# Batch 0's scores formed twice and one exponential per part, batch 1's mask added by TensorE

## The chip, the cores and the metric

The kernel runs on one core of a Trainium2 chip. The metric is the device time of one execution in microseconds (us). Every time below comes from timed runs or from one profiled execution. PE is the matrix engine (TensorE), DVE is VectorE, ACT is ScalarE, POOL is GpSimd, SP issues the DMAs.

## The reference

Three parts follow each other. Only the first is touched by the change.

```python
# q, k, v: 4 batches x 8 heads x 576 positions x 64
scores = (1/8) * q @ k.T
# heads 0..3: keys within 32 positions before the query (local)
# heads 4..7: earlier keys with the same position modulo 32 (strided)
scores = np.where(mask, scores, -1e9)
scores = scores - scores.max(-1)
attn = np.exp(scores); attn /= attn.sum(-1) + 1e-9
x = (attn @ v)                       # becomes 2304 tokens x 512
...
h = x @ w_in                         # 512 x 2048
g = h * sigmoid(1.702 * h)
x = g @ w_out                        # 2048 x 512
...
# soft mixture: 8 experts of 4 slots each, over all 2304 tokens
```

## The kernel before, in words

**Attention.** Heads go in pairs, `hp` = 0 to 3; pairs 0 and 1 are local, 2 and 3 strided (with positions permuted so that the keys a query needs are dense). Every pair has two parts. `att_scores(b, hp, part)` forms one part's scores in one PSUM bank: 5 or 4 tiles of 96 keys for a local pair (480 or 384 columns), 6 or 5 tiles of 64 keys for a strided one (384 or 320 columns), each tile with two small f32 matmuls for the pair's heads (L162). Then DVE takes the negated maximum of each row (L175), ACT takes the exponential of each tile with that maximum as bias and sums its row (L180), DVE adds 1e-9 and inverts (L181, L182), and POOL multiplies (L183). Batches differ in the mask. In batch 0 (`early`) a bf16 matmul with the identity writes eight times the mask into the bank first (L155, L157) and the scores accumulate on it; the maximum and the exponentials read PSUM. In the other batches DVE scales the scores and adds the mask on the way to SBUF (L165). `att_transpose` transposes the probabilities on PE and copies them out, in batch 0 alternately by DVE (L200) and ACT (L202); `att_values` multiplies with the values and splits the result into two tensors for the next product (L242 on ACT, L243 on DVE).

**Order of attention.** `attention_steps(b)` gives scores of the first parts, then scores, transposes and values in turn. Batch 0 runs at the start, before the expert layer. After each of its score steps one filler matmul is issued, and four after each other step (`keep_busy`, L78: bf16, 512 columns, their result is not used). Batches 1, 2 and 3 run beside chunks 0, 1 and 2 of the layer that follows, one step at a time.

**The layer.** The 2304 tokens are cut into chunks of 512, 512, 512, 512 and 256. For each chunk, 16 steps `f` each form 128 hidden units by 12 matmuls (`gemm1`, L312) and their activation (L315 on ACT, L316 on DVE). In chunk 0 the weights come along: `load_w` (L260 on ACT, L261 on POOL, L262 to L264 on DVE) converts a pair of 64-bit tiles to f32 two steps ahead, `split` (L271 on ACT, L272 on POOL) cuts a weight into two parts, `wo_transpose` (L279) and `wo_phi` (L287) prepare the logits, which L331 forms. `load_w` for f = 0 and 1 and `split(0)` are issued within batch 0's attention. Conversion tiles have four buffers, raw tiles three; scores, transposes, values and several others share five PSUM banks (`ps_m`). After the chunks come the experts, whose 28 MB of weights are loaded when chunk buffers come free.

**Order on the engines.** Semaphores and the order of instructions on each engine come from a planner, which starts from the program's order and reorders by its own costs. An engine then executes its list in that order.

Of the kernel before, what the change touches and what calls it, by code (L numbers as in the profile page):

```python
# [13 lines left out]
AF = mybir.ActivationFunctionType  # L14
ALU = mybir.AluOpType
AX = mybir.AxisListType
# [12 lines left out]
SCALE = 0.125  # L29
# [12 lines left out]
def tile_kernel(ctx: ExitStack, tc: tile.TileContext, lqk, lv, sqk, sv, wraw, phi, wexp, cst, out):  # L42
    nc = tc.nc
    P = 128
# [20 lines left out]
    def mtile(name):  # L65
        return ps_m.tile([P, 512], F32, tag="m", name=name)
# [16 lines left out]
    ident = cs[:, C_ID:C_ID + 128]  # L83
# [3 lines left out]
    identb = att.tile([P, P], BF16, name="identb", bufs=1)  # L87
    maskb = att.tile([P, C_END - C_ML], BF16, name="maskb", bufs=1)
    maskL, maskL0, maskS = maskb[:, :KL], maskb[:, KL:2 * KL], maskb[:, 2 * KL:]
# [39 lines left out]
    def att_scores(b, hp, part):  # L129
        t = qkv[b, hp]  # L130
        local = hp < 2
        nk, step = (KL, QT) if local else (KS, QS)
        ko = S if local else SW
        total, half = (NTL, 5) if local else (NTS, HS)
        u0, u1 = (0, half) if part == 0 else (half, total)
        nt = u1 - u0
        early = b == 0
        nm = f"{b}_{hp}_{part}"
        if part == 0:
            shape = [P, NTL if local else 2 * HS, nk]  # L140
            if b == 0 and hp >= 2:
                ts = ep.tile(shape, F32, name=f"ts_{b}_{hp}")
            else:
                ts = att.tile(shape, F32, tag="ts", name=f"ts_{b}_{hp}")
            probs[b, hp] = ts
            if not local:
                nc.gpsimd.memset(ts[:, NTS], 0.0)
        if local:
            ts = probs[b, hp][:, u0:u1]
        else:  # L150
            ts = probs[b, hp].rearrange("p (j e) k -> p e j k", e=2)[:, part, :nt]
        sp = mtile(f"s_{nm}")[:, :nt * nk].rearrange("p (u k) -> p u k", k=nk)
        mask = maskL if local else maskS
        if early:
            nc.tensor.matmul(sp, identb, mask.unsqueeze(1).to_broadcast([P, nt, nk]), start=True, stop=False)  # L155
            if local and part == 0:
                nc.tensor.matmul(sp[:, 0], identb, maskL0, start=False, stop=False)  # L157
        for u in range(nt):
            qo = step * (u0 + u)
            for h in range(2):  # L160
                hs = slice(64 * h, 64 * h + 64)
                nc.tensor.matmul(sp[hs, u], t[hs, qo:qo + 64], t[hs, ko + qo:ko + qo + nk], start=not early, stop=not early or u == nt - 1)  # L162

        def add_mask(a, z, m):
            nc.vector.scalar_tensor_tensor(ts[:, a:z], sp[:, a:z], SCALE, m.unsqueeze(1).to_broadcast([P, z - a, nk]), op0=ALU.mult, op1=ALU.add)  # L165

        if not early:
            if local and part == 0:
                add_mask(0, 1, maskL0)
                add_mask(1, nt, mask)  # L170
            else:
                add_mask(0, nt, mask)
        nmx = att.tile([P, 6], F32, tag="nmx", name=f"nmx_{nm}", bufs=4)
        src, sc = (sp, SCALE) if early else (ts, 1.0)
        nc.vector.tensor_reduce(nmx[:, :nt], src, axis=AX.X, op=ALU.max, negate=True)  # L175
        if early:
            nc.vector.tensor_scalar_mul(nmx[:, :nt], nmx[:, :nt], SCALE)
        sm = att.tile([P, 6], F32, tag="sm", name=f"sm_{nm}", bufs=4)
        for u in range(nt):
            nc.scalar.activation(ts[:, u], src[:, u], AF.Exp, scale=sc, bias=nmx[:, u:u + 1], accum_out=sm[:, u:u + 1])  # L180
        nc.vector.tensor_scalar_add(sm[:, :nt], sm[:, :nt], 1e-9)  # L181
        nc.vector.reciprocal(sm[:, :nt], sm[:, :nt])  # L182
        nc.gpsimd.tensor_tensor(ts, ts, sm[:, :nt].unsqueeze(2).to_broadcast([P, nt, nk]), op=ALU.mult)  # L183

    def att_transpose(b, hp):
        ts = probs.pop((b, hp))
        local = hp < 2
        nk, groups = (KL, ((0, 3), (3, 6), (6, 9))) if local else (P, ((0, 3), (3, 6)))
        if b == 0 and hp % 2:
            pt = ep.tile([P, groups[-1][1], P], F32, name=f"pt_{b}_{hp}")  # L190
        else:
            pt = att.tile([P, groups[-1][1], P], F32, tag="pt", name=f"pt_{b}_{hp}", bufs=1)
        ptiles[b, hp] = pt
        for n, (a, z) in enumerate(groups):
            ptp = mtile(f"ptp_{b}_{hp}_{n}")[:, :P * (z - a)].rearrange("p (u q) -> p u q", q=P)
            for u in range(a, z):
                src = ts[:, u] if local else ts[:, 2 * u:2 * u + 2].rearrange("p e k -> p (e k)")
                nc.tensor.transpose(ptp[:nk, u - a], src, ident)  # L198
            if n % 2 == 0 and b == 0:
                nc.vector.tensor_copy(pt[:nk, a:z], ptp[:nk])  # L200
            else:
                nc.scalar.copy(pt[:nk, a:z], ptp[:nk])  # L202

    def att_values(b, hp):
        pt, v = ptiles.pop((b, hp)), vals[b, hp]
# [272 lines left out]
    def attention_steps(b):  # L478
        la = 2 if b else 4
        order = list(range(la)) + [x for u in range(la, 8) for x in (la - 1 - u, u)] + list(range(la - 9, -9, -1))  # L480
        for x in order:
            if x >= 0:
                if b and x % 2 == 0:
                    load_qk(b, x // 2)
                att_scores(b, x // 2, x % 2)
                if b == 0:
                    keep_busy(1)
            else:
                x = -x - 1
                if x % 2:  # L490
                    att_values(b, x // 2)
                else:
                    if b:
                        load_v(b, x // 2)
                    att_transpose(b, x // 2)
                if b == 0:
                    keep_busy(4)
            yield
# [286 lines left out]
```

## Time and profile before

| | |
|---|---|
| time, median of 3 runs | 447.37 us (446.51 to 449.94) |
| time of the profiled execution | 446.48 us |
| its span, first to last instruction | 444.7 us |
| busy: PE, DVE, ACT, POOL | 415.2, 264.7, 189.4, 77.6 us |
| granted TensorE clock, mean | 0.98 of full |

Busy times are sums over a core whose engines work side by side, and a matmul counts as busy until its modelled end, also when it is held up. The span is 1.8 us shorter than the time of the execution.

### The profile page before, as it was taken

Reading aid. Unit: us, or ns where it says so; the run is one execution under the profiler, and the core shown is the slowest. Engines: PE = TensorE matmul, PEld = TensorE weight load, DVE = VectorE, ACT = ScalarE, POOL = GpSimd, SP = SyncE. Lnnn points to the kernel's source line nnn. Section 1 sums busy time; section 2 is a strip of 40 time slices with the busy share of each in tenths; the row PEclk is TensorE's granted clock in tenths of the full one; section 3 lists DMA queues with packets and bytes.
Section 4 is the critical chain, followed back from the end, with each engine's and each line's share of the span. In section 5 each row is a group of like instructions: output and inputs, shape, how many; then the busy total and the mean of one; then the engine's idle time right before and its main releaser. Section 6 shows DMA issues by size and latency. Waiting matters only on the chain.

```text
span 444.7 us, 9668 instructions
## 1 busy us (share of the span) xinstructions
PE 415.2 (93%) x3896; PEld 287.2 (65%) x3902; DVE 264.7 (60%) x564; ACT 189.4 (43%) x619; POOL 77.6 (17%) x96
## 2 busy tenths in 40 slices
PE   8877999998879999999999999999999999699964
PEld 3655786766557776776675867875777797243533
DVE  2589999988876565545656556545545464622213
ACT  1885776766555553445462436331221222020212
POOL 0354454535451100010010001000000000010000
PEclk9999999999898999999999999999999999999995
DMA  8956667584762120212503101570001899999998
GB/s 233 364 163 220 243 183 271 172 314 148 251 199 65 57 76 23 91 35 64 185 1 97 34 5 38 182 291 1 1 0 44 336 357 310 363 346 425 420 386 281
DMA packets 23229, 80.88 MB, mean 182 GB/s; under 512 B 2064, under 2 KB 7056, under 8 KB 19088
## 3 DMA queue, kind: packets, MB, share of 16 engines
q1 hardware_dynamic: 23184, 80.26, 50.8%
q8 instruction: 31, 0.51, 0.5%
q14 instruction: 14, 0.11, 0.1%
HBM read 71.34 MB, written 8.91 MB: 180 GB/s over the span
## 4 chain that ended last, share of the span: by engine, by line
PE 71%; DMA 9%; DVE 8%; ACT 4%; POOL 4%; issue 2%; SPq 0%; ACTq 0%; POOLq 0%
PE h L312 42%; DMA ex<-wexp 7%; PE lg L331 5%; PE u L416 4%; PE s L162 4%; PE ptp L198 3%; PE wp L287 3%; PE av L217 2%; DVE wc L263 2%; ACT ts L180 2%; DMA qk<-lqk 2%; POOL wi L272 2%; PE wot L279 1%; POOL ts L183 1%; DVE wc L264 1%
## 5 line engine op out<-in xcount | busy, mean ns | idle before, releaser
L312 PE MATMUL h<-x,wi 128*128 128x512 f32 (+1 forms) x960 | 224.7, 381 | 5.9 <-POOL wi L272 3.5
L312 PEld LDWEIGHTS h<-x,wi 128*128 128x128 f32 x960 | 162.7, 190 | 53.5 <-issue 13.8
L316 DVE SCALAR_TENSOR_TENSOR gT<-gT,h 128x512 f32<-128x512 f32 (+1 forms) x64 | 40.5, 633 | 61.8 <-ACT gT L315 61.4
L315 ACT ACTIVATE gT<-h 128x512 f32<-128x512 f32 (+1 forms) x64 | 35.6, 556 | 69.7 <-PE h L312 69.5
L180 ACT ACTIVATE ts<-ts,nmx 128x64 f32<-128x64 f32 (+1 forms) x120 | 41.6, 349 | 29.5 <-DVE nmx L175 29.2
L183 POOL TENSOR_TENSOR ts<-ts,sm 128x384 f32<-128x384 f32 (+2 forms) x32 | 28.1, 880 | 139.5 <-DVE sm L182 65.4
L339 DVE STREAM_TRANSPOSE gT<-gT 128x512 f32<-128x512 f32 (+1 forms) x64 | 41.0, 649 | 0.8
L261 POOL TENSOR_SCALAR wc<-wc 128x512 f32<-128x512 f32 x32 | 24.3, 759 | 32.9 <-ACT wc L260 32.7
L263 DVE SCALAR_TENSOR_TENSOR wc<-raw,wc 128x512 uint32<-128x512 uint32 x32 | 28.0, 878 | 0.3
L264 DVE SCALAR_TENSOR_TENSOR wc<-raw,wc 128x512 uint32<-128x512 uint32 x32 | 26.7, 834 | 0.1
L331 PE MATMUL lg<-gT,wp 128*32 128x512 f32 (+1 forms) x128 | 26.4, 564 | 0.0
L162 PE MATMUL s<-qk 64*64 64x96 f32 (+1 forms) x552 | 24.8, 235 | 0.8 <-DMA qk<-lqk 0.8
L272 POOL TENSOR_TENSOR wi<-wc,wi 128x512 fp32r<-128x512 f32 x16 | 22.5, 1406 | 16.2 <-ACT wi L271 15.8
L162 PEld LDWEIGHTS s<-qk 64*64 64x64 f32 x552 | 20.9, 133 | 6.7 <-issue 4.7
L202 ACT COPY pt<-ptp 96x384 f32<-96x384 f32 (+1 forms) x34 | 15.1, 482 | 20.5 <-PE ptp L198 20.3
L262 DVE TENSOR_SCALAR wc<-wc 128x512 uint32<-128x512 uint32 x32 | 17.3, 544 | 10.6 <-POOL wc L261 10.5
L242 ACT CAST x<-av 128x320 fp32r<-128x320 f32 (+20 forms) x54 | 19.1, 399 | 10.3 <-DVE x L243 8.9
L181 DVE TENSOR_SCALAR sm<-sm 128x5 f32<-128x5 f32 (+2 forms) x32 | 7.1, 222 | 26.7 <-ACT ts L180 26.5
L180 ACT ACTIVATION_READ_ACCUMULATOR ts<-ts,nmx 128x1 f32 x120 | 22.6, 188 | 0.0
L198 PE MATMUL ptp<-cs,ts 128*96 128x128 f32 (+1 forms) x120 | 18.3, 286 | 4.1 <-POOL ts L183 3.0
L416 PE MATMUL u<-gT,dT 32*32 32x512 f32 x576 | 20.2, 597 | 1.9 <-DVE z L396 1.9
L260 ACT ACTIVATE wc<-raw 128x512 f32<-128x512 f32 x32 | 21.6, 679 | 0.2 <-DMA raw<-wraw 0.2
(112 smaller groups left out, 457.7 us busy)
## 6 DMA issues: line engine op xcount, KB each, us to landing
ex<-wexp SPq DMA_DIRECT2D x28, 1024.0 KB, 8.2
raw<-wraw SPq DMA_DIRECT2D x32, 512.0 KB, 3.9
qk<-lqk SPq DMA_DIRECT2D x8, 592.0 KB, 4.2
wo_scr<-wc SPq DMA_DIRECT2D x16, 256.0 KB, 2.4
ex<-wo_scr SPq DMA_DIRECT2D x4, 1024.0 KB, 6.9
gT<-wexp SPq DMA_DIRECT2D x4, 1024.0 KB, 5.9
out<-gT SPq DMA_DIRECT2D x8, 512.0 KB, 4.1
qk<-sqk SPq DMA_DIRECT2D x6, 604.0 KB, 4.2
```

The costliest lines, as they stand in the source:

```text
L162: nc.tensor.matmul(sp[hs, u], t[hs, qo:qo + 64], t[hs, ko + qo:ko + qo + nk], start=not early, stop=not early or u == nt - 1)
L180: nc.scalar.activation(ts[:, u], src[:, u], AF.Exp, scale=sc, bias=nmx[:, u:u + 1], accum_out=sm[:, u:u + 1])
L183: nc.gpsimd.tensor_tensor(ts, ts, sm[:, :nt].unsqueeze(2).to_broadcast([P, nt, nk]), op=ALU.mult)
L198: nc.tensor.transpose(ptp[:nk, u - a], src, ident)
L263: nc.vector.scalar_tensor_tensor(u, raw[:, :, 1], 0xC0000000, u, op0=ALU.bitwise_and, op1=ALU.bitwise_or)
L272: nc.gpsimd.tensor_tensor(w[:, 1], t, w[:, 0].bitcast(F32), op=ALU.subtract)
L312: nc.tensor.matmul(h[:, :N], w[:, we, 128 * kt:128 * kt + 128], x[xe][:, kt, :N], start=n == 0, stop=n == 11)
L315: nc.scalar.activation(g[:, :N], h[:, :N], AF.Tanh, scale=0.851)
L316: nc.vector.scalar_tensor_tensor(g[:, :N], g[:, :N], 1.0, h[:, :N], op0=ALU.add, op1=ALU.mult)
L331: nc.tensor.matmul(lgs[c][32 * j:32 * j + 32, :N], wp[:, f0 + j, :], gs[c, f0 + j][:, :N], start=f0 == 0, stop=f0 == NF - 4)
L339: nc.vector.transpose(t_slots(c)[:, f, :N], gs[c, f][:, :N])
L416: nc.tensor.matmul(us[a][32 * j:32 * j + 32, :].rearrange("p (t f) -> p t f", f=32), dT[q, 32 * b:32 * b + 32], gT[q, :, 32 * b:32 * b + 3 ...
```

## The change

In batch 0 (`whole`) a part's mask and scores are formed once for the maximum and then a second time into another bank, onto which a matmul with the f32 identity adds the negated maximum, spread over each tile's columns. ACT takes one exponential over the whole part, and DVE sums the rows. The eight small multiplications of the maximum by 1/8 leave batch 0. In batch 1 the mask is added by TensorE as batch 0 had it, and maximum and exponentials read PSUM; these parts get the small multiplication. In batches 1 to 3 the 1e-9 is added by POOL. All copies of transposed probabilities go to ACT.

```diff
-        early = b == 0
+        early, whole = b < 2, b == 0
...
+        def scores(name, last):
+            sp = mtile(name)[:, :nt * nk].rearrange("p (u k) -> p u k", k=nk)
+            if early:
+                nc.tensor.matmul(sp, identb, mask.unsqueeze(1).to_broadcast([P, nt, nk]), start=True, stop=False)
+                if local and part == 0:
+                    nc.tensor.matmul(sp[:, 0], identb, maskL0, start=False, stop=False)
+            for u in range(nt):
+                qo = step * (u0 + u)
+                for h in range(2):
+                    hs = slice(64 * h, 64 * h + 64)
+                    nc.tensor.matmul(sp[hs, u], t[hs, qo:qo + 64], t[hs, ko + qo:ko + qo + nk], start=not early, stop=not early or (last and u == nt - 1))
+            return sp
+
+        sp = scores(f"s_{nm}", True)
...
-        if early:
-            nc.vector.tensor_scalar_mul(nmx[:, :nt], nmx[:, :nt], SCALE)
         sm = att.tile([P, 6], F32, tag="sm", name=f"sm_{nm}", bufs=4)
-        for u in range(nt):
-            nc.scalar.activation(ts[:, u], src[:, u], AF.Exp, scale=sc, bias=nmx[:, u:u + 1], accum_out=sm[:, u:u + 1])
-        nc.vector.tensor_scalar_add(sm[:, :nt], sm[:, :nt], 1e-9)
+        if whole:
+            sp = scores(f"t_{nm}", False)
+            nc.tensor.matmul(sp, ident, nmx[:, :nt].unsqueeze(2).to_broadcast([P, nt, nk]), start=False, stop=True)
+            nc.scalar.activation(ts, sp, AF.Exp, scale=SCALE)
+            nc.vector.tensor_reduce(sm[:, :nt], ts, axis=AX.X, op=ALU.add)
+            nc.vector.tensor_scalar_add(sm[:, :nt], sm[:, :nt], 1e-9)
+        else:
+            if early:
+                nc.vector.tensor_scalar_mul(nmx[:, :nt], nmx[:, :nt], SCALE)
+            for u in range(nt):
+                nc.scalar.activation(ts[:, u], src[:, u], AF.Exp, scale=sc, bias=nmx[:, u:u + 1], accum_out=sm[:, u:u + 1])
+            nc.gpsimd.tensor_scalar_add(sm[:, :nt], sm[:, :nt], 1e-9)
...
-            if n % 2 == 0 and b == 0:
-                nc.vector.tensor_copy(pt[:nk, a:z], ptp[:nk])
-            else:
-                nc.scalar.copy(pt[:nk, a:z], ptp[:nk])
+            nc.scalar.copy(pt[:nk, a:z], ptp[:nk])
```

## Rows read from the trace of the kernel before

**Rows 1.** Windows: stretch, length; busy PE, PEld, DVE, ACT, POOL; clock; DMA.

```profile
6.69:20.00 13.31, 11.72 (x176) 8.09 (x178) 5.95 (x20) 9.57 (x50) 4.08 (x5) 1.00 1.02 350
20.00:42.67 22.67, 16.75 (x243) 11.60 (x241) 20.68 (x46) 16.02 (x62) 10.30 (x13) 1.00 0.60 195
42.67:100.00 57.33, 56.10 (x448) 41.33 (x447) 53.68 (x100) 39.38 (x123) 27.55 (x31) 1.00 0.69 237
100.00:144.42 44.42, 38.98 (x298) 27.92 (x300) 34.61 (x62) 24.13 (x69) 19.04 (x19) 0.92 0.51 166
144.42:344.00 199.58, 199.41 (x1804) 144.31 (x1804) 109.89 (x230) 80.91 (x275) 14.09 (x20) 1.00 0.20 67
```

**Rows 2.** Groups by line, 6.69 to 42.67 us: busy us, mean ns | idle before.

```profile
L180 ACT ACTIVATE ts<-s,nmx 128x64 f32<-128x64 f32 (+1 forms) x40 | 12.4, 347 | 1.6 <-DVE nmx L177 1.3 <-issue 0.2
L78 PE MATMUL busy<-busy 128*128 128x512 bf16 x33 | 9.1, 385 | 0.5 <-issue 0.3 <-PE av L217 0.2
L175 DVE TENSOR_REDUCE nmx<-s 128x5 f32<-128x480 f32 (+3 forms) x8 | 4.5, 561 | 5.1 <-PE s L162 5.1
L200 DVE COPY pt<-ptp 96x384 f32<-96x384 f32 (+1 forms) x6 | 3.3, 546 | 1.9 <-PE ptp L198 1.9
L177 DVE TENSOR_SCALAR nmx<-nmx 128x5 f32<-128x5 f32 (+2 forms) x8 | 1.7, 214 | 0.1
```

**Rows 3.** Timeline of PE and DVE in batch 0: start us, us.

```profile
6.69 0.37 PE L155 MATMUL s<-maskb,identb 128*128 128x480 bf16 x1
...
8.01 0.34 PE L155 MATMUL s<-maskb,identb 128*128 128x384 bf16 x1
...
8.27 0.88 PE L162 MATMUL s<-qk 64*64 64x96 f32 x16
...
25.53 0.30 PE L155 MATMUL s<-maskb,identb 128*128 128x320 bf16 x1
...
26.49 0.39 PE L78 MATMUL busy<-busy 128*128 128x512 bf16 x1
...
26.79 1.65 DVE L263 SCALAR_TENSOR_TENSOR wc<-raw,wc 128x512 uint32<-128x512 uint32 x1
...
28.36 0.48 DVE L175 TENSOR_REDUCE nmx<-s 128x5 f32<-128x320 f32 x1
...
31.46 0.43 DVE L262 TENSOR_SCALAR wc<-wc 128x512 uint32<-128x512 uint32 x1 [0.95 <-POOL wc L261]
...
31.92 0.69 DVE L263 SCALAR_TENSOR_TENSOR wc<-raw,wc 128x512 uint32<-128x512 uint32 x1
```

**Rows 4.** Groups by line, 42.67 to 144.42 us.

```profile
L165 DVE SCALAR_TENSOR_TENSOR ts<-s,maskb 128x384 f32<-128x384 f32 (+2 forms) x10 | 4.6, 476 | 3.6 <-PE s L162 3.6
...
L181 DVE TENSOR_SCALAR sm<-sm 128x5 f32<-128x5 f32 (+2 forms) x8 | 2.3, 293 | 0.1
```

**Rows 5.** The chain of waits from 122 us on: start us, us, what.

```profile
122.72 0.62 ACT wi L271
...
129.88 0.62 ACT wi L271
...
140.93 0.63 PE wot L279 x4
...
142.49 0.88 PE wp L287 x8
...
144.38 1.63 PE s L162 x36
146.01 2.95 PE h L312 x12
...
154.89 1.06 PE lr L380 x2
...
159.57 1.20 PE av L217 x36
...
172.87 1.12 PE ptp L198 x9
```

More of the change, by code (lines that the diff above doesn't have):

```diff
@@ L151, in att_scores @@
             ts = probs[b, hp].rearrange("p (j e) k -> p e j k", e=2)[:, part, :nt]
-        sp = mtile(f"s_{nm}")[:, :nt * nk].rearrange("p (u k) -> p u k", k=nk)
         mask = maskL if local else maskS
-        if early:
-            nc.tensor.matmul(sp, identb, mask.unsqueeze(1).to_broadcast([P, nt, nk]), start=True, stop=False)
-            if local and part == 0:
-                nc.tensor.matmul(sp[:, 0], identb, maskL0, start=False, stop=False)
-        for u in range(nt):
[L159 to L162, printed above, removed]
+        def scores(name, last):
[11 more added lines that the diff above has]
+        sp = scores(f"s_{nm}", True)
         def add_mask(a, z, m):
@@ L175, in att_scores @@
         nc.vector.tensor_reduce(nmx[:, :nt], src, axis=AX.X, op=ALU.max, negate=True)
-        if early:
-            nc.vector.tensor_scalar_mul(nmx[:, :nt], nmx[:, :nt], SCALE)
         sm = att.tile([P, 6], F32, tag="sm", name=f"sm_{nm}", bufs=4)
-        for u in range(nt):
-            nc.scalar.activation(ts[:, u], src[:, u], AF.Exp, scale=sc, bias=nmx[:, u:u + 1], accum_out=sm[:, u:u + 1])
-        nc.vector.tensor_scalar_add(sm[:, :nt], sm[:, :nt], 1e-9)
+        if whole:
[10 more added lines that the diff above has]
+            nc.gpsimd.tensor_scalar_add(sm[:, :nt], sm[:, :nt], 1e-9)
         nc.vector.reciprocal(sm[:, :nt], sm[:, :nt])
```

## The prediction

> **What bounds the kernel now.** I read the windows first, stage by stage [rows 1]. They split the run into four. From 6.69 us, where the first scores start, to 42.67 us, where the first expert-layer product (`gemm1` of chunk 0, f = 0) ends, no engine is full over the whole stretch: PE is busy 11.72 + 16.75 = 28.5 of 36.0 us, so 7.5 us idle; DVE idles until 20 us and is at 20.68 of 22.67 after it. From 42.67 to 144.42 us (chunk 0 with the weight conversion and batch 1's attention beside it) DVE is at 53.68 + 34.61 = 88.3 of 101.75 us and PE, on paper, at 95.1. From 144.42 to 344 us PE is full (199.4 of 199.6), and in the tail to 444.7 us the expert weights are loaded and used. The change adds work to PE in the first stage and takes work off DVE and ACT in the first two; chunks 1 to 4 only shift by what the first two stages lose or win, and so does the tail, whose loads start when chunk buffers come free. So the question is when chunk 0 ends.
>
> In the first stage the groups by line [rows 2] show what the change aims at: 40 exponentials of 347 ns on ACT, and six copies and eight reductions of about 0.55 us on DVE. They also show 33 filler matmuls (`keep_busy`, L78): these are issued in program order like all else, the change keeps them, and PE has to run them. So PE's slack is the 7.5 us of idle time and not the fillers.
>
> In chunk 0, "busy" overstates PE: a matmul that waits counts until it ends. A product of 12 matmuls takes 2.95 us alone [rows 5]. The chain of waits [rows 5] shows the pace there in two ways. Part of it runs through DVE's conversions; part is a loop: ACT's cast of a weight tile (122.72), POOL's subtraction, PE's product and `wo_phi`, and only then ACT's next cast (129.88), 7.16 us for one step with no DVE in it. The mean step is (144.42 - 42.67) / 15 = 6.78 us.
>
> **First stage, PE.** Each of batch 0's eight parts repeats its mask and scores and adds one f32 matmul with the identity. Scores, start to start [rows 3]: 8.01 - 6.69 = 1.32 us for the first local part, 26.49 - 25.53 = 0.96 us for the last strided one. The other two forms have 384 columns, between these; I put them at an estimated 1.1 us each. Twice the four forms: 2 x 4.48 = 9.0 us. The identity matmul is not in this trace. The nearest row is the f32 product of 512 columns with a 128x128 operand, two records in 1.06 us [rows 5]; the four forms have 480, 384, 384 and 320 columns, 1568 in all, and each comes twice: 2 x 1568 / 512 x 1.06 = 6.5 us. From below it is bounded by the single-record products of the expert layer, 2.95 / 12 = 0.246 us for 512 columns, which gives 1.5 us. I take 6.5, because the row at 154.89 has the same operand types as the new matmul. Added: 15.5 us. Against 7.5 us of idle time that leaves **+8.0 us** at the end of the first product, if PE fills every hole (low end 9.0 + 1.5 - 7.5 = +3.0).
>
> The new matmul waits for DVE's reduction, and matmuls queued behind it wait too. A reduction takes 0.561 us on average [rows 2], less than the repeated scores of 0.96 to 1.32 us, so these cover it where DVE is free. For the last part it was not [rows 3]: the scores were out at about 26.49, a conversion of 1.65 us stood in front (26.79), the reduction ran from 28.36 to 28.84. That is 2.35 us against a cover of 0.96, so 1.4 us of parking. For the seven others I estimate some 0.6 us together, from the same stage's DVE being less full before 20 us. Up to 2.0 us in all; I take none, because DVE has fewer copies and a conversion may go earlier, and keep +10.0 as the high end.
>
> **First stage, ACT and DVE.** ACT loses 40 exponentials (12.4 us, and the reads of their sums) and gains eight of up to 480 columns; its cast of 512 columns takes 0.62 us [rows 5], so at most about 8 x 0.62 = 5.0 us, and six copies, which took 0.546 us on DVE. That is some 4 us or more off ACT, all beside a PE that is now the later engine: worth nothing by itself, but it lets the first casts of raw weights go earlier. DVE loses six copies (3.3 us) and eight small multiplications (1.7) and gains eight sums over the same shapes as the maxima (4.5 us for eight): -0.5 us, nothing. The first exponential moves behind the first identity matmul, by the repeat and that matmul some 2.3 us; this lies under the scores that PE still has to do.
>
> **Chunk 0.** Batch 1 loses ten mask additions on DVE, 4.6 us, and eight additions of 1e-9, 2.3 us [rows 4]; it gains eight multiplications of 0.214 us [rows 2], 1.7 us. DVE: **-5.2 us**, at full worth where DVE sets the pace. The 1e-9 goes to POOL, which is idle more than half of this stage (27.55 + 19.04 = 46.6 of 101.75 us). There it queues behind conversions, but POOL's next multiplication of the same part had to wait for the same exponentials anyway, so little new waits. PE gains ten mask matmuls: 8.27 - 8.01 = 0.26 us each [rows 3], 2.6 us. From the chain, a step needs 2.95 + 0.63 + 0.88 us, 15 of them 66.9; attention of one local pair 1.63 + 1.20 + 1.12 = 3.95, four pairs at most 15.8; I allow 3 us for logits. That is 85.7 of 101.75 us, 16 us of slack, and the 2.6 us lie in it. If that cover is gone, they count.
>
> A score bank of batch 1 is now held until its exponentials are done instead of until the mask is added, some 2 us longer by a reduction of 0.561 and up to six exponentials of 0.347 us [rows 2], out of five banks; nothing in the chain waits for a bank by name, so I cost it at nothing.
>
> **Head start.** With ACT free earlier and PE late, one more weight pair can be converted before the first product. DVE needs for each of its two tiles 0.43 us (31.46) and 0.69 us twice (31.92; the third operation is of the same form) [rows 3], 3.6 us for the pair; the four buffers of the conversion allow one such pair. Between 0 and -3.6 I take half: **-1.8 us**.
>
> **Batches 2 and 3** only send the 1e-9 through POOL. They run under a PE that is full [rows 1]; nothing.
>
> The sum is made against the profiled execution, whose time was 446.48 us with a span of 444.7: 446.5 + 8.0 - 5.2 - 1.8 = **447.5 us**. The median of the runs, 447.37, is 0.9 above that execution, the same within what it can tell: a change of under 1%, 442.9 to 451.8, can't be told from none.
>
> **Rivals.** *Slower: the lost time is never won back.* The place is the loop of 7.16 us through ACT's cast and POOL's subtraction. If it, and not DVE, sets most of chunk 0's steps, 5.2 us off DVE buy nothing and the first stage's high end stands: 446.5 + 10.0 = 456.5 us; should the masks fall into the loop, 2.6 more. It decides once the step stays at 6.78 us or more. For it: between 100 and 144.42 us DVE is at only 34.61 of 44.42 us. Against: from 42.67 to 100 us it is at 53.68 of 57.33 [rows 1]. On the parking in it the Trainium skill has a rule (TensorE: Matmul & The Clock Gate, "The mechanism"): matmuls start and end in program order, only weight loads are pulled ahead, so nothing that is ready behind a waiting identity matmul can pass it. By that rule the 2.0 us are lost in full, 449.5 us in place of the sum's 447.5 if the rest holds; no run here shows such a matmul yet.
>
> *Faster: chunk 0 runs at PE's pace.* PE then needs 85.7 + 2.6 = 88.3 us from 42.67 + 8.0 = 50.7, so chunk 0's last product ends at 139.0 instead of 144.42: 446.5 - 5.4 = 441.1 us, and down to 436 with the cheap identity matmul. It decides if the step falls below about 6.2 us. For it: DVE then has 83 us of work in 88. Against: the loop, and two nearly full engines feeding each other.
>
> *The change doesn't do what it says:* if the new instructions end up in an order in which PE idles as before in the first stage, the 15.5 us count nearly whole, and it is the slow case or worse.
>
> **How the numbers follow.** Forecast 0.42, with its own range 446.5 + 3.0 - 5.2 - 3.6 = 441 to 446.5 + 10.0 - 5.2 = 451; the fast rival 0.30, the slow one 0.28. Of the forecast's 0.42 some 0.04 lie below 442.9 and 0.01 above 451.8: faster 0.34, same 0.37, slower 0.29. Leaving one in ten off either end gives 438 to 457.
>
> **What would show it.** The first product's tanh at about 50.7 us instead of just after 42.67; PE idle under 2 us between 6.69 us and there; the identity matmul near 0.8 us for 384 columns; ACT's batch-0 exponentials at eight of under 0.6 us. In chunk 0: DVE about 83 us, the step at 6.3 us, the tanh of f = 15 near 145. The prediction is wrong if the first product is not late (the identity matmul is cheap, or the fillers vanish into waits), or if the step of chunk 0 does not move.

## The result, and the profile after

The changed kernel took 454.97 us (median of 4 runs, 450.86 to 456.35). Beside the kernel before, the ratio is 1.015 [1.0104, 1.0196]: 1.5% slower, where no change that can be told was forecast. That is above the forecast's own range (441 to 451 us) and inside the wide one (438 to 457); the sum was 7.5 us short, and slower had been given 0.29. The profiled execution took 454.01 us with a span of 452.2, 7.5 us more than before's.

The windows of the changed kernel come first, with the columns of [rows 1]: the two stretches of the first stage there, then the first stage to the end of its first product (gemm1 of f = 0, now at 60.01 us), to the tanh of f = 1, from there to the tanh of f = 15, and 2 us in the middle.

```profile
6.69:20.00 13.31, 13.31 (x167) 8.58 (x166) 5.93 (x15) 2.25 (x5) 2.90 (x4) 1.00 0.96 338
20.00:42.67 22.67, 19.65 (x301) 13.26 (x299) 19.23 (x41) 11.12 (x25) 12.57 (x14) 1.00 0.65 226
6.69:60.01 53.32, 48.64 (x649) 33.29 (x648) 34.79 (x77) 22.45 (x56) 19.73 (x22) 0.97 0.64 220
6.69:64.14 57.45, 52.77 (x674) 36.92 (x673) 36.44 (x81) 25.82 (x70) 22.82 (x27) 0.97 0.63 220
64.14:150.29 86.15, 81.72 (x687) 60.86 (x686) 73.05 (x129) 54.60 (x162) 41.12 (x47) 1.00 0.62 200
52.00:54.00 2.00, 2.00 (x8) 1.78 (x7) 0.97 (x4) 1.31 (x4) 0.00 (x0) 0.50 0.52 154
```

The same two last stretches of the kernel before, which [rows 1] do not cut at these points:

```profile
6.69:50.86 44.17, 36.66 (x484) 26.78 (x488) 34.72 (x84) 31.42 (x133) 16.19 (x20) 1.00 0.72 247
50.86:144.42 93.56, 86.89 (x672) 62.16 (x672) 80.20 (x143) 57.68 (x168) 44.77 (x47) 0.96 0.61 204
```

Read them as a balance. The tanh of f = 1 comes 13.3 us later (64.14 after 50.86). Up to it PE does 52.77 - 36.66 = 16.1 us more, and idles 57.45 - 52.77 = 4.7 us instead of 7.5, which gives back 2.8; 16.1 - 2.8 = 13.3. Then chunk 0 gives back 7.4 us: its fourteen steps from f = 1 to f = 15 take 86.15 us instead of 93.56. So the tanh of f = 15 is 5.9 us late (150.29 after 144.42), and the rest adds 1.6.

What PE does in addition shows in its groups by line from 6.69 to 60.01 us of the changed kernel:

```profile
L78 PE MATMUL busy<-busy 128*128 128x512 bf16 x38 | 11.1, 398 | 0.0
L184 PE MATMUL t<-nmx,cs 128*128 128x384 f32 (+2 forms) x16 | 7.4, 545 | 3.0 <-DVE nmx L180 3.0
...
L164 PE MATMUL t<-qk 64*64 64x96 f32 x72 | 3.8, 248 | 0.0
...
L164 PE MATMUL t<-qkv 64*64 64x64 f32 x88 | 3.4, 222 | 0.0
L157 PE MATMUL t<-maskb,identb 128*128 128x384 bf16 (+2 forms) x8 | 2.7, 340 | 0.0
```

The identity matmul (L184) is two records per part, as the price of [rows 5] had it: 7.4 us of busy time, which overlaps its neighbours a little. The repeated scores and masks (t) are 9.9 us here and another 0.4 in the smaller mask matmuls, which are not shown. The fillers (L78) are still there, 11.1 us.

Where PE stayed idle is in the list of its waits, 6.69 to 55 us (total us, times, longest):

```profile
PE t L184 <- DVE nmx L180: 3.0, 2, 1.6
...
PE av L226 <- ACT pt L211: 1.6, 1, 1.6
```

That is nearly the whole 4.7 us. The timeline of the first identity matmul and around the three holes (start us, us):

```profile
9.51 1.07 PE L184 MATMUL t<-nmx,cs 128*128 128x480 f32 x2
...
31.19 0.81 PE L184 MATMUL t<-nmx,cs 128*128 128x320 f32 x2 [1.39 <-DVE nmx L180]
...
41.18 1.04 DVE L271 TENSOR_SCALAR wc<-wc 128x512 uint32<-128x512 uint32 x1 [0.37 <-POOL wc L270]
42.14 0.48 DVE L180 TENSOR_REDUCE nmx<-s 128x5 f32<-128x320 f32 x1
...
42.68 0.81 PE L184 MATMUL t<-nmx,cs 128*128 128x320 f32 x2 [1.64 <-DVE nmx L180]
...
47.04 0.68 ACT L269 ACTIVATE wc<-raw 128x512 f32<-128x512 f32 x1 [1.81 <-POOL wi L281]
47.61 1.35 ACT L251 CAST x<-av 128x224 fp32r<-128x224 f32 x3
49.35 0.22 ACT L251 CAST x<-av 128x36 fp32r<-128x36 f32 x1 [0.39 <-DVE x L252]
49.44 0.87 ACT L211 COPY pt<-ptp 128x384 f32<-128x384 f32 x2
...
49.98 0.27 PE L226 MATMUL av<-pt,qkv 54*64 54x54 f32 x2 [1.65 <-ACT pt L211]
```

At 42.68 it is the pattern of [rows 3]: a conversion on DVE stands in front of the reduction, and PE is parked at the identity matmul. At 49.98 it is one of the copies that moved to ACT: the transposes ran on PE from 46.64 us, but the copy stood in ACT's queue behind the cast of a raw weight (0.68 us), three casts of x (1.35 us) and a fourth that waited 0.39 us for DVE. Behind this hole the granted clock fell to 0.50 between 52 and 54 us (windows above).

In front of all that, ACT's exponentials have become cheap without gain, as the groups by line from 6.69 to 55.5 us show:

```profile
L185 ACT ACTIVATE ts<-t 128x384 f32<-128x384 f32 (+2 forms) x8 | 4.0, 498 | 21.8 <-PE t L184 21.8
```

Forty exponentials of 12.4 us [rows 2] are now eight of 4.0 us, and ACT stands idle 21.8 us before them, waiting for PE.

### The profile page after: what moved, and what is told of

Its sections match the earlier page's. It is cut to its first block, busy times and chain, and to the rows that moved or that the text cites. A ratio compares the mean times of both kernels' runs of the same rounds, so it can differ in the third digit from the quotient of the medians.

```text
span 452.2 us, 9956 instructions
## 1 busy us (share of the span) xinstructions
PE 427.2 (94%) x4098; PEld 296.3 (66%) x4098; DVE 256.3 (57%) x532; ACT 182.1 (40%) x553; POOL 84.3 (19%) x120
## 4 chain that ended last, share of the span: by engine, by line
PE 66%; DVE 10%; DMA 7%; POOL 7%; ACT 6%; issue 3%; POOLq 0%; ACTq 0%; SPq 0%
PE h L321 38%; DMA ex<-wexp 7%; PE u L425 4%; PE s L164 4%; PE lg L340 3%; ACT ts L192 3%; POOL wi L281 2%; PE ptp L210 2%; PE av L226 2%; DVE wc L272 2%; DVE wc L273 2%; POOL ts L195 2%; PE busy L78 2%; POOL wc L270 2%; PE wp L296 1%
## 5 line engine op out<-in xcount | busy, mean ns | idle before, releaser
L321 PE MATMUL h<-x,wi 128*128 128x512 f32 (+1 forms) x960 | 221.7, 379 | 1.2 <-POOL wi L281 1.1
L192 ACT ACTIVATE ts<-ts,nmx 128x64 f32<-128x64 f32 (+1 forms) x80 | 27.7, 348 | 26.7 <-DVE nmx L180 26.4
L270 POOL TENSOR_SCALAR wc<-wc 128x512 f32<-128x512 f32 x32 | 23.8, 744 | 28.9 <-ACT wc L269 26.3
L193 POOL TENSOR_SCALAR sm<-sm 128x5 f32<-128x5 f32 (+2 forms) x24 | 6.7, 277 | 118.4 <-ACT ts L192 118.1
L271 DVE TENSOR_SCALAR wc<-wc 128x512 uint32<-128x512 uint32 x32 | 20.1, 629 | 11.1 <-POOL wc L270 11.1
L194 DVE RECIPROCAL sm<-sm 128x5 f32<-128x5 f32 (+2 forms) x32 | 6.0, 186 | 36.1 <-POOL sm L193 35.6
L273 DVE SCALAR_TENSOR_TENSOR wc<-raw,wc 128x512 uint32<-128x512 uint32 x32 | 25.3, 791 | 0.2
L272 DVE SCALAR_TENSOR_TENSOR wc<-raw,wc 128x512 uint32<-128x512 uint32 x32 | 24.3, 759 | 0.3
L340 PE MATMUL lg<-gT,wp 128*32 128x512 f32 (+1 forms) x128 | 23.3, 564 | 0.0
L686 POOL MEMSET hz<- 128x512 f32 x4 | 2.1, 560 | 111.9 <-DMA gT<-wexp 111.9
L296 PEld LDWEIGHTS wp<-phs,woT 128*128 128x128 f32 x128 | 15.9, 193 | 9.8 <-ACT woT L290 8.7
L252 DVE TENSOR_TENSOR x<-av,x 128x320 fp32r<-128x320 f32 (+20 forms) x54 | 19.5, 390 | 4.4 <-ACT x L251 4.3
```

The lines of the kernel that those rows point to most:

```text
L270: nc.gpsimd.tensor_scalar(t, t, F64_LARGE, F64_SMALL, op0=ALU.min, op1=ALU.max)
L272: nc.vector.scalar_tensor_tensor(u, raw[:, :, 1], 0xC0000000, u, op0=ALU.bitwise_and, op1=ALU.bitwise_or)
L273: nc.vector.scalar_tensor_tensor(u, raw[:, :, 0], 29, u, op0=ALU.logical_shift_right, op1=ALU.bitwise_or)
L321: nc.tensor.matmul(h[:, :N], w[:, we, 128 * kt:128 * kt + 128], x[xe][:, kt, :N], start=n == 0, stop=n == 11)
L340: nc.tensor.matmul(lgs[c][32 * j:32 * j + 32, :N], wp[:, f0 + j, :], gs[c, f0 + j][:, :N], start=f0 == 0, stop=f0 == NF - 4)
```

## The experiments

Two questions stood open: what made the first stage 13.3 us late and not 8.0, and what gave 7.4 us back in chunk 0: batch 1's relief of DVE, as forecast, or the lateness itself. Theory: PE's added work and its unfilled holes set the first stage; chunk 0's early end is the stream of weight conversions, which runs on while PE is late, so some lateness is free. The last part of this theory did not hold, as the runs below show. The rival is the forecast's own account, where DVE's relief shortens the step.

**One half each.** Batch 0 as before and batch 1 changed:

```diff
-        early, whole = b < 2, b == 0
+        early, whole = b < 2, False
...
-            nc.gpsimd.tensor_scalar_add(sm[:, :nt], sm[:, :nt], 1e-9)
+            (nc.gpsimd if b else nc.vector).tensor_scalar_add(sm[:, :nt], sm[:, :nt], 1e-9)
...
-            nc.scalar.copy(pt[:nk, a:z], ptp[:nk])
+            if n % 2 == 0 and b == 0:
+                nc.vector.tensor_copy(pt[:nk, a:z], ptp[:nk])
+            else:
+                nc.scalar.copy(pt[:nk, a:z], ptp[:nk])
```

> Only batch 1's mask by TensorE and the 1e-9 of batches 1 to 3 on POOL; batch 0 as before. Theory (the first stage loses PE time, chunk 0 wins DVE time, and the two parts add): 440 us, 437 to 443, since the loss of 13 to 14 us in the first stage is gone and the 7 us won in chunk 0 stay; tanh of f = 1 near 51 us, of f = 15 near 137. Rival (the planner's new order of chunk 0 makes the time, whatever the parts): 446 to 455, and the steps of chunk 0 no shorter than 6.6 us.

Measured: ratio 1.0044 [1.0008, 1.008]. The tanh of f = 1 is at 50.89 us, where it was before, and f = 15 at 143.17: 1.25 us won in chunk 0, not 5.2, and none of it left at the end. That is the rival's time; the theory's 437 to 443 us missed.

The other half, batch 0 changed (with all copies on ACT) and batch 1 as before:

```diff
-        early, whole = b < 2, b == 0
+        early, whole = b == 0, b == 0
...
-            nc.gpsimd.tensor_scalar_add(sm[:, :nt], sm[:, :nt], 1e-9)
+            nc.vector.tensor_scalar_add(sm[:, :nt], sm[:, :nt], 1e-9)
```

> Only batch 0's part of the change and its copies on ACT; batches 1 to 3 as before. Theory (parts add): the first stage 13 us later and chunk 0 at the old pace or a little under it because of conversions done early: 458 us, 455 to 461. Rival (the gain in chunk 0 comes from the later start, conversions being ahead, and not from batch 1's mask): 453 to 456, as the whole change.

Measured: 1.0127 [1.0064, 1.0191], as slow as the whole change, which is the rival. f = 1 at 60.68, f = 15 at 147.41: 86.73 us for the fourteen steps, with batch 1's work still on DVE. The windows of this kernel between the two:

```profile
60.68:147.41 86.73, 81.91 (x686) 61.93 (x688) 79.59 (x138) 57.07 (x166) 41.24 (x44) 1.00 0.60 199
```

DVE is at 79.59 us, as in the kernel before (80.20), and yet the steps are nearly as short as in the changed kernel (86.15, with DVE at 73.05). DVE's relief is not what shortened them.

**Batch 1's mask alone**, without the 1e-9 on POOL (batch 0 as in the first run):

```diff
-            (nc.gpsimd if b else nc.vector).tensor_scalar_add(sm[:, :nt], sm[:, :nt], 1e-9)
+            nc.vector.tensor_scalar_add(sm[:, :nt], sm[:, :nt], 1e-9)
```

> As the run with batch 1 only, but the 1e-9 stays on DVE: the mask by TensorE alone. Theory (taking work off DVE buys nothing in chunk 0, since a step there waits for a chain through several engines): 447 to 449.5, like the kernel before. Rival (the mask does buy some 4 us, and the trip over POOL, DVE's reciprocal waiting for it, gave them back): 443 to 446.

Measured: 1.0096 [1.0055, 1.0136]; f = 1 at 52.20, f = 15 at 148.42, 96.2 us between them. Theory and rival both missed: the mask on PE by itself costs. With the 1e-9 on POOL it was 1.0044; the two intervals overlap (1.0055 to 1.008), so that moving the 1e-9 helps is likely and not settled.

**Lateness alone.** The kernel before, with 64 more filler matmuls in batch 0 and nothing else:

```diff
                 if b == 0:
-                    keep_busy(1)
+                    keep_busy(9)
```

> The kernel before with nine filler matmuls instead of one after each of batch 0's eight score steps: 64 x 0.213 = 13.6 us more work for PE in the first stage and nothing else. Theory (chunk 0 wins back a late start by itself, because conversions get ahead while PE is late): second tanh 8 to 13 us later than 50.9 us, then steps of 6.2 instead of 6.7 us, so that about 6 are won back: 453 us, 451 to 455. Rival (the shorter steps come from batch 0's exponentials and copies having left ACT and DVE): steps stay at 6.7 us, the delay stays whole: 457 to 461.

Measured: 1.0149 [1.0075, 1.0222]. f = 1 at 62.54, 11.7 us late; f = 15 at 149.99, 5.6 us late. Its windows:

```profile
6.69:62.54 55.85, 49.92 (x535) 31.75 (x531) 35.36 (x89) 32.56 (x135) 19.06 (x23) 0.94 0.66 227
62.54:149.99 87.45, 83.47 (x686) 62.95 (x688) 79.72 (x138) 57.11 (x166) 40.78 (x44) 0.98 0.60 198
```

PE is busy 13.3 us longer up to the tanh of f = 1 (49.92 after 36.66), and the steps after it take 87.45 us. Not all of that is filler work: the granted clock is 0.94 over the stretch, and PE stands idle 5.0 us before a copy on DVE (L200). The time, a median of 455.85 us, lies just above the theory's 451 to 455 and under the rival's 457. With no line of the change in it, this kernel shows the change's picture: late by 12 at f = 1, half of it given back by f = 15. Lateness by itself brings the shorter steps.

It does not do so by conversions that get ahead. The last of DVE's operations on a weight tile, eighth and ninth in the kernel before, then ninth and tenth in the changed one:

```profile
50.34 0.65 DVE L264 SCALAR_TENSOR_TENSOR wc<-raw,wc 128x512 uint32<-128x512 uint32 x1
55.98 0.68 DVE L264 SCALAR_TENSOR_TENSOR wc<-raw,wc 128x512 uint32<-128x512 uint32 x1
...
57.52 0.68 DVE L273 SCALAR_TENSOR_TENSOR wc<-raw,wc 128x512 uint32<-128x512 uint32 x1
66.61 0.65 DVE L273 SCALAR_TENSOR_TENSOR wc<-raw,wc 128x512 uint32<-128x512 uint32 x1
```

By the tanh of f = 1 (50.86 and 64.14 us) eight tiles are converted or being finished in the one and nine in the other: one tile more in 13.3 us. And nothing is given back at first. Cut at the tanh of f = 9, the fourteen steps fall into two stretches, here for the kernel before, the changed one and the one with more fillers:

```profile
50.86:99.92 49.06, 47.91 (x374) 34.24 (x372) 45.52 (x82) 33.47 (x101) 25.73 (x28) 1.00 0.70 238
99.92:144.42 44.50, 38.98 (x298) 27.92 (x300) 34.69 (x62) 24.21 (x69) 19.04 (x19) 0.92 0.51 167
...
64.14:112.67 48.53, 46.25 (x391) 36.23 (x389) 42.08 (x73) 31.86 (x98) 23.06 (x29) 1.00 0.67 213
112.67:150.29 37.62, 35.47 (x298) 24.63 (x298) 30.97 (x56) 22.75 (x64) 18.06 (x19) 1.00 0.55 184
...
62.54:111.06 48.52, 47.09 (x387) 37.61 (x387) 44.41 (x78) 32.64 (x99) 21.93 (x26) 0.96 0.61 202
111.06:149.99 38.93, 36.37 (x300) 25.34 (x302) 35.31 (x61) 24.48 (x68) 18.85 (x19) 1.00 0.59 192
```

Eight steps take 49 us in all three. The last six take 44.50 us in the kernel before and 37.62 in the changed one, with the same 298 matmuls on PE. The 6.9 us are 3.5 us more of busy time on PE in the kernel before, where the granted clock is 0.92 and not 1.00, and 3.4 us more of idle time (5.52 against 2.15). By this estimate about half of what is given back is the clock, and half are waits. In the kernel before, 4.7 of its 5.5 us of waits there are for ACT's cast and POOL's subtraction of a weight (L271, L272). Why the late kernels have fewer of them there was not tried.

**The identity matmul in one record.** The changed kernel, with the negated maximum and the identity in F32R, the type of the expert layer's products; the maximum is rounded by it:

```diff
+    identr = att.tile([P, P], F32R, name="identr", bufs=1)
...
-        nmx = att.tile([P, 6], F32, tag="nmx", name=f"nmx_{nm}", bufs=4)
+        nmx = att.tile([P, 6], F32R if whole else F32, tag="nmx", name=f"nmx_{nm}", bufs=4)
...
-            nc.tensor.matmul(sp, ident, nmx[:, :nt].unsqueeze(2).to_broadcast([P, nt, nk]), start=False, stop=True)
+            nc.tensor.matmul(sp, identr, nmx[:, :nt].unsqueeze(2).to_broadcast([P, nt, nk]), start=False, stop=True)
...
+    nc.vector.tensor_copy(identr, ident)
```

> The whole change, with the negated maximum rounded to the type of the expert layer's products, so that the identity matmul is one record. The maximum is only a shift of each row, so its rounding changes the result little. Theory (PE's work sets the first stage): the eight matmuls fall from about 0.85 us to 0.25 us apart, 4.5 us less: 450 us, 448 to 452. Rival (the waits for DVE's reduction set it): no change, 453 to 456.

Measured: 0.9996 [0.9966, 1.0026], a little faster than the theory's 448 to 452 us; the loss is gone. f = 1 at 57.32, f = 15 at 143.44. Its groups by line from 6.69 to 55.5 us:

```profile
L185 PE MATMUL t<-nmx,identr 128*128 128x384 f32 (+2 forms) x8 | 3.5, 433 | 1.1 <-DVE nmx L181 1.1
```

3.5 us instead of 7.4, and 1.1 us of parking instead of 3.0. There is no fall of the clock up to f = 1 here:

```profile
6.69:57.32 50.63, 46.07 (x650) 33.26 (x656) 33.98 (x80) 24.90 (x69) 21.36 (x25) 1.00 0.72 251
```

Of the 6.8 us that f = 1 gains over the changed kernel, PE's busy time explains 6.7 (52.77 - 46.07): 3.9 are the identity matmul, some 1.2 the slow clock (last section), and the rest was not traced. PE's idle time stayed at 4.6 us (50.63 - 46.07), since waits for ACT and POOL took the place of the parking.

**Without fillers.** The changed kernel less the 40 filler matmuls that stand between batch 0's steps:

```diff
-                if b == 0:
-                    keep_busy(1)
...
-                if b == 0:
-                    keep_busy(4)
```

> The whole change without the 40 filler matmuls of batch 0's attention (the ten at the start stay). Theory (PE's work sets the first stage, fillers count as work): 32 fillers of 0.213 us, 6.8 us less, 448 us, 446 to 451. Rival (the clock falls when PE waits without fillers, or the fillers only fill waits): 453 to 458, with a granted clock under 0.9 somewhere between 20 and 55 us.

Measured: 1.0035 [0.9998, 1.0071]; f = 1 at 52.48, f = 15 at 143.86. The median of 449.18 us is in the theory's range. In the changed kernel the fillers delay f = 1 by 11.7 us. The same edit in the kernel before:

> The kernel before without the 40 fillers of batch 0's attention. Theory (before, the first stage waits for ACT and DVE, fillers lie in PE's holes): same time, 446 to 449 us, with the second tanh near 50 us; a granted clock below 1 may cost up to 3 us. Rival (fillers were in the way before, too): 442 to 445.

Measured: 0.9974 [0.9936, 1.0012], a median of 448.99 us and so the theory's; f = 1 at 48.43, f = 15 at 144.36. There they delayed f = 1 by 2.4 us and cost nothing that can be told: f = 15 is where it was. But they did something else, which the windows to the tanh of f = 1 show, first of this kernel, then of the changed one without fillers:

```profile
6.69:48.43 41.74, 32.81 (x438) 25.13 (x437) 31.32 (x76) 27.68 (x115) 15.83 (x19) 0.84 0.69 234
...
6.69:52.48 45.79, 42.57 (x623) 30.55 (x623) 34.41 (x78) 24.09 (x67) 19.80 (x23) 1.00 0.76 257
```

Without them the granted clock of the kernel before falls to 0.84 in this stage, where it was 1.00. In the changed kernel it stays at 1.00, with PE busy 42.57 of 45.79 us by its own work.

**Both** edits on the changed kernel, the one-record identity matmul (with `identr` and the type of `nmx` as above) and no fillers:

```diff
-            nc.tensor.matmul(sp, ident, nmx[:, :nt].unsqueeze(2).to_broadcast([P, nt, nk]), start=False, stop=True)
+            nc.tensor.matmul(sp, identr, nmx[:, :nt].unsqueeze(2).to_broadcast([P, nt, nk]), start=False, stop=True)
...
-                if b == 0:
-                    keep_busy(1)
...
-                if b == 0:
-                    keep_busy(4)
```

> The whole change with the one-record identity matmul and without the 40 fillers. Theory (both take PE work from the first stage; part of what is won is lost again in chunk 0, as a later start was partly won back): 444 to 447, less than the 13 us that the two gained one by one. Rival (the gains add): 441 to 443.

Measured: 0.9905 [0.9868, 0.9941], as the theory had it and the lowest ratio of the study; f = 1 at 51.99, f = 15 at 142.02.

**The same without batch 1's part.** First the batch 0 half with the one-record identity matmul (`identr` and `nmx` again as above), fillers kept:

```diff
-        early, whole = b < 2, b == 0
+        early, whole = b == 0, b == 0
...
-            nc.gpsimd.tensor_scalar_add(sm[:, :nt], sm[:, :nt], 1e-9)
+            nc.vector.tensor_scalar_add(sm[:, :nt], sm[:, :nt], 1e-9)
...
-            nc.tensor.matmul(sp, ident, nmx[:, :nt].unsqueeze(2).to_broadcast([P, nt, nk]), start=False, stop=True)
+            nc.tensor.matmul(sp, identr, nmx[:, :nt].unsqueeze(2).to_broadcast([P, nt, nk]), start=False, stop=True)
```

> Batch 0's part alone with the one-record identity matmul. Theory (batch 1's part is worth nothing either way): 447 to 448.5, as the whole change with that matmul. Rival (batch 1's part buys some 3 us or more once PE isn't late): 450 or more.

Measured: 1.0015 [0.998, 1.0051], against 0.9996 with batch 1's part: the same, as the theory said. f = 1 at 57.99, f = 15 at 144.82. Then the fastest kernel with batch 1's mask on DVE again (the 1e-9 still on POOL):

```diff
-        early, whole = b < 2, b == 0
+        early, whole = b == 0, b == 0
```

> Batch 0 as in the whole change with the one-record identity matmul and without fillers; batch 1's mask stays on DVE as before; the 1e-9 of batches 1 to 3 on POOL. Theory (batch 1's mask on TensorE costs when chunk 0 starts early, POOL's 1e-9 helps): 441 to 444 us. Rival (with this start the mask is worth nothing either way): 444 to 446.

Measured: 0.9935 [0.9914, 0.9955], against 0.9905. Its median of 446.72 us lies above both ranges, but the kernel before stood at 449.49 us beside it; 0.9935 of 447.37 would be 444.5, the rival's. f = 1 at 54.84, f = 15 at 143.76. Neither pair tells a gain from batch 1's part.

**What holds chunk 0's end at 142 to 145 us.** The suspect was the ring of three buffers for raw weight tiles: a load can't start before a conversion on DVE has released a buffer. The kernel before with two buffers:

```diff
-    rawp = raw_es.enter_context(tc.tile_pool(name="rawp", bufs=3, side="right"))
+    rawp = raw_es.enter_context(tc.tile_pool(name="rawp", bufs=2, side="right"))
```

> The kernel before with two raw tiles instead of three, nothing else. Theory (ring of raw tiles): trips of 8 us at the least, two tiles per trip, steps of 8 us or more: 465 to 475 us. Rival (the ring has slack): 447 to 452.

Measured: 1.083 [1.078, 1.088], slower than the theory's 465 to 475 us, and the rival's slack is not there. f = 1 at 50.88 as before, f = 15 at 181.30, 36.9 us late. The waits of SP's queue from 64 to 140 us, in this kernel:

```profile
SPq L249 <- DVE wc L264: 50.5, 15, 8.0
```

and in the kernel before:

```profile
SPq L249 <- DVE wc L264: 23.8, 9, 3.7
```

The raw loads (L249) wait for a release on DVE for 50.5 of 76 us, before for 23.8. With four buffers, and one buffer fewer for the conversion in exchange for the memory:

```diff
-    rawp = raw_es.enter_context(tc.tile_pool(name="rawp", bufs=3, side="right"))
+    rawp = raw_es.enter_context(tc.tile_pool(name="rawp", bufs=4, side="right"))
...
-            t = rawp.tile([P, 512], F32, tag="wc", name=f"wc_{f}_{k}", bufs=4)
+            t = rawp.tile([P, 512], F32, tag="wc", name=f"wc_{f}_{k}", bufs=3)
```

> The kernel before with four raw tiles and three conversion tiles instead of three and four (there is no room for four and four). Theory (chunk 0 is paced by the ring of three raw tiles, load, ACT, POOL, three times DVE, then the next load, 10.1 us per trip and so 6.7 us for the two tiles of a step): one more tile shortens the step by up to 0.6 us until DVE or PE is full, 440 to 445 us, unless the third conversion tile was needed. Rival (raw tiles don't pace it): 447 to 452.

Measured: 1.0026 [0.9996, 1.0057]; f = 1 at 49.53, f = 15 at 141.74. The tanh of f = 15 comes 2.7 us earlier in that profile, the time is no better, as the rival said. Fewer buffers set the pace; whether three do was not isolated, since a conversion buffer was taken away with it.

## Where the prediction held and where it failed

All runs but the one with two raw tiles, in order of the tanh of f = 1, give the rule that it lacked (us):

| kernel | f = 1 | f = 15 | between | ratio |
|---|---|---|---|---|
| before, no fillers | 48.43 | 144.36 | 95.9 | 0.9974 |
| before, four raw and three conversion tiles | 49.53 | 141.74 | 92.2 | 1.0026 |
| before | 50.86 | 144.42 | 93.6 | 1 |
| batch 1 only | 50.89 | 143.17 | 92.3 | 1.0044 |
| changed, one record, no fillers | 51.99 | 142.02 | 90.0 | 0.9905 |
| batch 1's mask only | 52.20 | 148.42 | 96.2 | 1.0096 |
| changed, no fillers | 52.48 | 143.86 | 91.4 | 1.0035 |
| batch 0 only, one record, no fillers, 1e-9 on POOL | 54.84 | 143.76 | 88.9 | 0.9935 |
| changed, one record | 57.32 | 143.44 | 86.1 | 0.9996 |
| batch 0 only, one record | 57.99 | 144.82 | 86.8 | 1.0015 |
| batch 0 only | 60.68 | 147.41 | 86.7 | 1.0127 |
| before, 64 more fillers | 62.54 | 149.99 | 87.5 | 1.0149 |
| changed | 64.14 | 150.29 | 86.2 | 1.015 |

Up to some 58 us the start of chunk 0 is free: f = 15 stays at 142 to 145 us, save with the mask alone. From there the steps don't get shorter than 86.1 to 87.5 us for fourteen, and f = 15 moves with f = 1. So the start of chunk 0 has some 7 us of slack in the kernel before. The rule is one for f = 15 and coarse: it comes from one execution of each kernel, and that was 3.7 us below the median time with the added fillers and 2.3 above it with one record and no fillers.

**The step that failed: "+8.0 us at the end of the first product, if PE fills every hole".** The product itself ended 17.3 us late (60.01 after 42.67), in part because batch 1's first scores and masks (55.51 to 57.90 us) now come ahead of its last eight matmuls; at f = 1, where the order evens out, it is 13.3. The added work was right: 15.5 us forecast, 16.1 measured, some 1.2 us of slow clock included. The holes were not filled: of 7.5 us idle, 4.7 stayed. Of that 3.0 us are parking on DVE's reduction, which the prediction had seen and priced at 2.0 at most, and then left out of its sum, hoping that a conversion would go earlier; 1.65 us are the wait for a copy on ACT, a move that was costed at nothing because ACT had become emptier. It had, but at that moment the copy stood behind the casts listed above.

The high end of the identity matmul was the right one, and a little low: 7.4 us against 6.5, with 1.07 us for 480 columns and 0.81 for 320. The Trainium skill (TensorE: Matmul & The Clock Gate, "The mechanism") states that matmuls start and end in program order; the trace agrees, with 1.39 and 1.64 us in which PE did nothing before two identity matmuls.

**Chunk 0's -5.2 us for DVE's relief** is not there. DVE's busy time per step fell, but the half of the change that brings it wins 1.25 us in chunk 0 and ends 0.4% slower, and the half without it has the same short steps. The premise, that work taken off DVE comes off chunk 0 in full, fell with the runs.

**The head start of -1.8 us** was one tile, half of a pair, and one tile is what the trace shows at f = 1. But it is not what gave the time back: the next eight steps were no shorter (48.53 us against 49.06), and lateness by fillers alone gave back 11.7 - 5.6 = 6.1 us. What the late kernels lack is the end of chunk 0 as [rows 1] show it, a clock of 0.92 from 100 to 144.42 us and 5.4 us of 44.4 in which PE is idle; the prediction priced neither. Both terms together were forecast at -7.0 and measured at -7.4, a hit by luck, since the first gave next to nothing and the second came from elsewhere. By the table, 8.0 us late would have put f = 1 at 58.9, still close to the free stretch, and f = 15 at about 58.9 + 86.2 = 145.1 (an estimate), near the forecast's 145. The 5.3 us more were past the slack and counted in full.

**The rivals.** The slow one came nearest in time (456.5 against 454.97), but its mechanism, lost time that is never won back, is refuted: 7.4 us were. The point from which it was to decide, a step of 6.78 us or more, wasn't reached: the mean step from f = 1 on is 6.15. That step is below the 6.2 us at which the fast rival was to decide, so chunk 0 did run near its fast pace, and the kernel was slower all the same: the rival had the steps start from a first product at 50.7 us, with all but 8.0 us of the first stage's work fitting into the holes.

Of the signs named, these were wrong: the first product's tanh (61.61 us and not 50.7), PE's idle time (4.7 us and not under 2), DVE's busy time in chunk 0 (74.70 us from 60.01 to 150.29, and not 83) and the tanh of f = 15 (150.29 and not 145). These were right: the identity matmul (0.91 us for 384 columns against 0.8), the exponentials under 0.6 us, and a shorter step (6.15 us against 6.3).

**Open.** What sets the floor of 86 us is not shown: PE is busy 81.1 to 83.5 us of it, but that counts waiting. Nor is it shown why the last six steps of the late kernels keep the clock at 1.00 and wait less. The times don't follow f = 15 alone: with no fillers, one record instead of two moved f = 1 by 0.5 us and f = 15 by 1.8, but the ratio from 1.0035 to 0.9905, so what makes the fastest kernel faster than the one before is not shown either. Nor is it settled why batch 1's mask on PE costs when it comes alone, nor the 1.6 us that the changed kernel loses after f = 15; from there to the end of the span the profiles in the table range from 300.3 to 303.5 us, and the one of before is at the low end.

## What to carry to other kernels

Idle time on an engine is cover for new work only if that work is ready when the hole comes; when the new instruction itself waits for another engine, price its parking into the sum, not into the range. Before a stage's delay is carried to the end, try how much of it arrives there: here some 7 us of lateness were free and the rest cost nearly in full, and a run that only adds delay shows that without the change. A mechanism that gives time back has to be found where the time is given back; here that was eight steps later than expected. Filler work that fills holes costs next to nothing (and here held the clock) until real work arrives; then it has to be priced as work (here 11.7 us at f = 1), and taking it out together with a cheaper form of the new instruction turned a loss of 1.5% into a gain of 0.95%.

## What the runs showed of the hardware

In the changed kernel the granted clock fell to 0.50 of full, the 1.2 GHz level, between 52 and 54 us. Before that PE had had a hole of 1.64 us that ended at 42.68 and one of 1.65 us that ended at 49.98, and in all only 4.7 us of idle time since 6.69 us. The timeline shows the price:

```profile
43.98 1.03 PE L78 MATMUL busy<-busy 128*128 128x512 bf16 x4
...
49.98 0.94 PE L226 MATMUL av<-pt,qkv 54*64 54x54 f32 x44 [1.65 <-ACT pt L211]
50.85 1.38 PE L78 MATMUL busy<-busy 128*128 128x512 bf16 x4
52.02 1.06 PE L288 MATMUL wot<-cs,wc 128*128 128x128 f32 x4
52.73 2.06 PE L321 MATMUL h<-x,wi 128*128 128x512 f32 x4
...
65.21 1.17 PE L321 MATMUL h<-x,wi 128*128 128x512 f32 x4
```

Four fillers take 1.38 us instead of 1.03 (43.98 us), four products 2.06 instead of 1.17 (65.21 us), some 1.2 us together. Behind the hole that ended at 42.68 there was no such price: the granted clock is 1.00 in all windows from 42.67 to 50 us. Why one and not the other was not tried. The identity matmul with both operands in F32R is one record of 0.433 us on average, where the plain one is two of 0.545.
